# Where the sums of seven pairs stand: at step 2.65 of the next pair or directly ahead of its first values' group

## The chip, the cores and the metric

The kernel runs on one core of a Trainium2 chip. The metric is the device time of one execution in microseconds (us). The engines are named as in the profile: PE multiplies matrices (TensorE), PEld is its weight load, DVE is VectorE, ACT is ScalarE, POOL is GpSimd, and SP is the queue from which almost all transfers are issued. The chip's working memory (SBUF) and the accumulators (PSUM) have 128 partitions.

## The reference

The program is an attention with a bucket mask, followed by a feed-forward network with a rational function in place of the usual activation. Queries, keys and values have shape 4 x 8 x 768 x 64. Each query and each key gets a six-bit bucket, the signs of its product with `proj`; a query attends only to keys of its own bucket.

```python
mask = q_bucket[:, :, :, None] == k_bucket[:, :, None, :]
scores = np.where(mask, scale * np.matmul(q, k.transpose(0, 1, 3, 2)), -1e9)
attn = np.exp(scores - np.max(scores, axis=-1, keepdims=True))
attn = attn / (np.sum(attn, axis=-1, keepdims=True) + 1e-09)
x = np.matmul(attn, v)            # then 3072 tokens of 512 values
h = x @ w_in                      # 512 -> 2048
P = a[0] + a[1]*h + a[2]*h*h + a[3]*h*h*h
Q = 1.0 + np.abs(b[0])*np.abs(h) + np.abs(b[1])*h*h
out = (P / (Q + 1e-6)) @ w_out    # 2048 -> 512
```

## The kernel before

**Tiling.** The 32 heads (4 batches of 8) are worked on as 16 pairs; a pair's two heads share the 128 partitions, 64 each. A pair has 12 steps. Step s makes the scores of 128 keys against one half (384) of the queries, for both heads: half = s // 6, key tile = s % 6. Operands are kept as a rounded high part and a low part. Tile names of the profile: `pss` is scores, `psm` row maxima, `psb` bucket bits, `pst` a transpose of the maxima, `psv` values, `psu` sums, `psh` and `pso` the two products of the feed-forward part.

**One step.** `scores` issues, for each head, two matmuls into one of the three PSUM buffers of tag "s" in pool `ps_b`; ACT then writes exp(scores / 8) to one of seven tiles `E`. POOL adds the exps of three key tiles into a partial sum `acc`, so that a pair has four of these (two halves, `PARTS` = 2 each). `maxstep` belongs to the pair after the next: two matmuls into one of two buffers of `ps_a`, and a maximum by DVE. These maxima become the shift that is subtracted inside the scores.

**Values.** After six steps, `values` issues 24 matmuls for the six exps, 64 columns wide, the two heads side by side in the array. `values_out` copies one column (`col`) and moves the half's result, `xo`, out of PSUM on ACT; `values_store` writes it to memory.

**Sums.** `sums` multiplies the four partial sums by a matrix of ones: 8 products, 16 matmuls in the profile, each 32 columns wide and four of them beside each other in the array. They go to a buffer of tag "s"; ACT copies it to `sr`, and `sums_store` writes that to memory. Every fourth pair `recips` reads the sums of a batch back and makes reciprocals.

**Order.** Every operation of every engine is pinned to program order (`Ordered`). The order is made by a plan: `at(p, s, f, ...)` files a call under the key 12 p + s, where s may be a fraction and may run past 12 into the next pair; all calls are then made in order of their keys. `MID` holds the keys of the middle pairs, `FIRST` and `LAST` those of the first and the last. So sums at 14.65 of pair p are issued at step 2.65 of pair p + 1. In `MID`, per pair: values' groups at 5.66 and 11.05, values_out at 8.5 and 14.5 (step 2.5 of the next pair), the stores of xo at 9 and 15, bits at 2.81 in even pairs, the cast of the k of the pair after next at 1.19, a weight cast at 14.29 (step 2.29 of the next pair).

**Feed-forward part.** It begins in pair 15 and runs 6 blocks of 512 tokens by 16 slices of `w_in`'s columns. `gemm` makes `psh`, ACT, DVE and POOL make the rational function, and `gemm2`, four steps later, adds to `pso`. After a block, `store` writes four tiles of output rows, `o`. Up to then a block's next tokens are loaded, with products `y` in the buffers `lo0` and `lo1` of pool `raw`, which in the attention part hold the low parts of q and k.

Of the kernel before, what the change touches and what calls it, by code (L numbers as in the profile page):

```python
# [7 lines left out]
F32 = mybir.dt.float32  # L8
# [10 lines left out]
P = 128  # L19
S = 768  # L20
HQ = 384
# [4 lines left out]
NPAIR = B * NHP  # L26
NB = 6
TOK = B * S
DM = 512
# [6 lines left out]
CLAMP = 2.0 ** 40  # L36
PINNED = ("tensor", "vector", "scalar", "gpsimd", "sync")
PARTS = 2
ACCS = 5

MID = dict(
    group=6, values=[0.66, 0.05], values_out=3.5, maxima=7.17,
    maxima_steps=[0, 1.15, 1.73, 2.64, 3.32, 5.08, 5.86, 6.98, 8.0, 8.84, 10.26, 11.37], sums=14.65, sums_store=17.37,
    high=[-0.41, 1.19], low=[1.06, 3.35], bits=2.81, penalties=4.05, high_move=1.9, maskrows=5.61, second_low=-2.2,
    second_high=2.69, load_v=10.99, shift_turn=8.61, shift_rows=8.82, load=9.0, recips=[20.0, 22.0, 23.0],
    weights=[[1.44, 4.0, 4.1, 5.09, 5.49, 7.11, 9.5, 9.75, 17.5], [8.05, 10, 10.65, 11.5, 12.38, 14.29, 16.34, 19.32, 21.22]],
# [18 lines left out]
    sums=16.96, wide=8, share=11, third=0, sums14=14.69, weights14=1.44, sumst14=22.46,  # L65
# [8 lines left out]
class Ordered:  # L74


    def __init__(self, tc, engines=PINNED):
        self.tc, self.pinned = tc, engines
# [24 lines left out]
@with_exitstack  # L103
def bucket_attention_then_rational_ffn(ctx, tc, qT, kT, v, proj, w_in, w_out, coef, consts, out):
    nc = Ordered(tc)
    nc.scalar.preload_act_table_set("natural_log_exp_and_others")

    cpool = ctx.enter_context(tc.tile_pool(name="cpool", bufs=1))
    dpool = ctx.enter_context(tc.tile_pool(name="dpool", bufs=1, space=DRAM))
    wpool = ctx.enter_context(tc.tile_pool(name="wpool", bufs=1))  # L110


    raw = ctx.enter_context(tc.tile_pool(name="raw", bufs=2))
    ps_b = ctx.enter_context(tc.tile_pool(name="ps_b", bufs=1, space=PSUM))
    QF, KF = {}, {}

    def load(p, queue=nc.sync):
        both = raw.tile([P, 2, S], F32, tag="raw", name=f"qkf{p}")
        for t, (F, src) in enumerate(((QF, qT), (KF, kT))):
            F[p] = both[:, t, :]  # L120
            queue.dma_start(F[p], src[p])

    load(0)
    prj = cpool.tile([P, 2, 32], F32, name="prj")
    nc.scalar.dma_start(prj, proj)
    cst = cpool.tile([P, 2 + P], F32, name="cst")
    nc.scalar.dma_start(cst, consts)
    ident = cst[:, 2 : 2 + P]
    load(1)
    ones = cpool.tile([P, 32], F32, name="ones")  # L130
    nc.vector.memset(ones, 1.0)
    ab = cpool.tile([P, 6], F32, name="ab")
    a0, a1, a2, a3, b0, b1 = (ab[:, i : i + 1] for i in range(6))
    absb1 = cpool.tile([P, 1], F32, name="absb1")
    qbias = cpool.tile([P, 1], F32, name="qbias")
    nc.vector.memset(qbias, 1.0 + 1e-6)

    x_d = [dpool.tile([P, S], F32, name=f"x_d{i}") for i in range(NPAIR)]
    s_d = [dpool.tile([2 * NHP, S], F32, name=f"s_d{i}") for i in range(B)]
    r_d = [dpool.tile([2 * NHP, S], F32, name=f"r_d{i}") for i in range(B)]  # L140

    wo_d = [dpool.tile([P, 2, DM], F32R, name=f"wo_d{i}") for i in range(NFC)]

    wi_hi = wpool.tile([P, NCC, DFF], F32R, name="wi_hi")
    wi_lo = wpool.tile([P, NCC, DFF], F32R, name="wi_lo")

    tokens = Tokens(tc, nc, raw, x_d, r_d)
    gemm = Gemm1(nc, ps_b, tokens, wi_hi, wi_lo)
    tail = ctx.enter_context(tc.tile_pool(name="tail", bufs=1))

    def coefficients():
        nc.sync.dma_start(ab, coef)
        yield
        nc.scalar.activation(absb1, b1, AF.Abs)
        yield

    early = ExitStack()
    right = ctx.enter_context(ExitStack())
    ffn = Ffn(tc, nc, tokens, gemm, wo_d, (a0, a1, a2, a3, b0, absb1, qbias), tail, out)

    def operands_to_terms():
        early.close()
        ffn.terms_pool(right)
        tokens.last_rows = ffn.tp

    tail.tile([P, 32], F32, tag="below", name="below")
    last = attention(tc, nc, raw, ps_b, tail, tokens, early, operands_to_terms, ffn, load, QF, KF, v, w_in, w_out, wo_d, ident, cst,
                     ones, prj, wi_hi, wi_lo, x_d, s_d, r_d, coefficients)
    ffn.rest(ctx, last)
# [3 lines left out]
def attention(ctx, tc, nc, raw, ps_b, tail, tokens, early, operands_to_terms, ffn, load, QF, KF, v, w_in, w_out, wo_d, ident, cst, ones, prj,  # L173
# [215 lines left out]
    def values_out(p, hf):  # L389
        ps = AV.pop((p, hf))  # L390
        col = sm.tile([P, 1], F32, tag="col", name=f"col{p}_{hf}")
        xo = AV[p, hf] = tail.tile([P, DM], F32, tag="xo", name=f"xo{p}_{hf}", bufs=2)[:, 0:HQ]
        nc.scalar.copy(col, ps[:, HQ : HQ + 1])
        nc.scalar.activation(xo, ps[:, 0:HQ], AF.Identity, bias=col)

# [3 lines left out]
    def sums(p):  # L399
        ps = ps_b.tile([P, 512], F32, tag="s", bufs=3, name=f"psu{p}")  # L400
        for k in range(PARTS):
            for hf in range(2):
                acc = ACC.pop((p, hf, k))
                for h in range(2):
                    o = 64 * h + 32 * hf
                    nc.tensor.matmul(ps[o : o + 32, 0:HQ], ones, acc[:, h, :], start=(k == 0), stop=(k == PARTS - 1))
        ACC[p] = tail.tile([P, DM], F32, tag="sr", name=f"sr{p}")[:, 0:HQ]
        nc.scalar.copy(ACC[p], ps[:, 0:HQ])

    def sums_store(p):  # L410
# [65 lines left out]
    def at(p, s, f, *args):  # L476
        plan.setdefault(12 * p + s, []).append((f, args))
# [5 lines left out]
    for p in range(NPAIR):  # L483
        mid = 0 < p < NPAIR - 1
        n = MID["group"] if mid else (FIRST if p == 0 else LAST)["group"]
        for s in range(12):
            if p > 0 or s >= FIRST["ahead"]:
                at(p, s, scores, p, s)

            if p > 1:  # L490
                at(p - 2, MID["maxima"] + MID["maxima_steps"][s] if p > 2 else FIRST["maxima2"] + FIRST["rate2"] * s, maxstep, p, s)
            if s % n == n - 1:
                for i in range(s - n + 1, s + 1):
                    at(p, s + (MID["values"][s // n] if mid else (FIRST if p == 0 else LAST)["values"][s // n]), values, p, i)
            if s % NT == NT - 1:
                at(p, s + (LAST["vout14"] if (p, s) == (NPAIR - 2, 11) else MID["values_out"] if mid else (FIRST if p == 0 else LAST)["values_out"]), values_out, p, s // NT)
        for hf in range(2):
            at(p, 6 * hf + 9, values_store, p, hf)
        if p < NPAIR - 1:
            at(p, MID["sums"] if p < NPAIR - 2 else LAST["sums14"], sums, p)  # L500
            at(p, MID["sums_store"] if p < NPAIR - 2 else LAST["sumst14"], sums_store, p)
        if p > 1:
            for t in range(2):
                at(p - 2, (MID if p > 2 else FIRST)["high"][t], high, p, t)
                at(p - 2, (MID if p > 2 else FIRST)["low"][t], low, p, t, nc.vector if p > 2 else nc.gpsimd)
            if p % 2 == 0:
                at(p - 2, (MID if p > 2 else FIRST)["bits"], bits, p)
                at(p - 2, (MID if p > 2 else FIRST)["penalties"], penalties, p)
            at(p - 2, (MID if p > 2 else FIRST)["high_move"], high_move, p)
            at(p - 2, (MID if p > 2 else FIRST)["maskrows"], maskrows, p)  # L510
        if p > 0:
            at(p - 1, (MID if p > 1 else FIRST)["second_low"], second_low, p)
            at(p - 1, (MID if p > 1 else FIRST)["second_high"], second_high, p)
            at(p - 1, (MID if p > 1 else FIRST)["load_v"], load_v, p)
        if p > 1:
            at(p - 1, MID["shift_turn"], shift_turn, p)
            at(p - 1, MID["shift_rows"], shift_rows, p)
        if p > 3:
            at(p - 4, MID["load"], load, p)
        if p % NHP == NHP - 1 and p + 1 < NPAIR:  # L520
            spread(p, MID["recips"], recips(p // NHP))
# [12 lines left out]
    for f, x in enumerate(LAST["ffn"]):  # L534
        at(NPAIR - 1, x, ffn.step, f)
    at(NPAIR - 1, LAST["sums"], sums, NPAIR - 1)

    warm(12)
    K1[0] = operand("k1", 0, [P, 2, S], F32R, 3)
# [124 lines left out]
class Ffn:  # L664
# [1 line left out]

    LAG = 4

    def __init__(self, tc, nc, tokens, gemm, wo_d, coef, rows, out):
        self.tc, self.nc, self.tokens, self.gemm, self.wo_d, self.coef, self.out = tc, nc, tokens, gemm, wo_d, coef, out  # L670
        self.rows = rows
        self.state, self.sums = {}, {}
        self.done = 0

# [57 lines left out]
    def store(self, t, i, end, last):  # L732
        nc = self.nc
        if end and last:
            o = self.tp.tile([P, DM], F32, tag="h2", name=f"o{t}_{i}", bufs=2)
        else:
            tag, bufs = ("sr", 1) if i % 3 == 2 else ("xo", 2)
            o = self.rows.tile([P, DM], F32, tag=tag, name=f"o{t}_{i}", bufs=bufs)
        if end and i == 1:
            nc.vector.tensor_scalar(out=o, in0=self.sums[t, i], scalar1=-1.0, scalar2=None, op0=ALU.mult)  # L740
        else:
# [88 lines left out]
```

## Time and profile before

| | us |
|---|---|
| median of 3 runs (929.65 to 930.06) | 929.81 |
| the profiled execution, own time | 929.79 |
| its span in the profile | 928.0 |
| PE busy | 920.8 (99%) |
| DVE busy | 842.0 (91%) |
| ACT busy | 647.6 (70%) |
| POOL busy | 435.8 (47%) |

The attention part takes some 400 us, the feed-forward part the rest. A PE that is busy 99% does not work at its peak: matmuls are pipelined, a row's duration is longer than the distance to the next start, and starts tell more than durations. The granted clock is full in all forty slices. In rows of a timeline the first number is the start in us from the span's start and the second the time to the end of the last of the merged instructions; brackets hold idle time before it and what ended that.

### The profile page before, as it was taken

The page shows a single profiled execution, that of the slowest core. Times are in us where ns is not written, and L with a number is a line of the kernel's source. Part 1 is how long each engine was busy: PE and PEld are TensorE (multiplying, and loading weights), DVE is VectorE, ACT ScalarE, POOL GpSimd, SP SyncE. Part 2 cuts the span into 40 slices and gives each one's busy share as a digit, 9 for nine tenths or more (in the row PEclk, how much of TensorE's full clock was granted, in tenths as well). Part 3 has the DMA queues.
Part 4 walks back from the last instruction along what each step waited for, and adds up shares of the span by engine and source line. Part 5 has one row for each costly group of instructions (what it writes and reads, how often), then busy time and mean ns, then how long its engine had stood idle before and what let it go on. Part 6 is the DMA issues. An engine that isn't in the chain of part 4 may idle for free.

```text
span 928.0 us, 13694 instructions
## 1 busy us (share of the span) xinstructions
PE 920.8 (99%) x4678; PEld 699.9 (75%) x4678; DVE 842.0 (91%) x1029; ACT 647.6 (70%) x1229; POOL 435.8 (47%) x361
## 2 busy tenths in 40 slices
PE   8999999999999999999999999999999999999998
PEld 4666766666767676668888888888888888888886
DVE  6799889888988898888998999899999999998996
ACT  6567767676767766887767766776676677667664
POOL 5587878787788877622222232223222322232221
PEclk9999999999999999999999999999999999999999
DMA  6767878878877777545402100400040003001001
GB/s 197 214 181 219 229 230 230 223 214 212 242 212 225 229 195 233 163 155 197 163 1 81 56 1 1 136 2 0 1 137 1 1 34 102 1 1 46 1 1 46
DMA packets 51098, 111.57 MB, mean 120 GB/s; under 512 B 9330, under 2 KB 19942, under 8 KB 51028
## 3 DMA queue, kind: packets, MB, share of 16 engines
q1 hardware_dynamic: 50596, 110.34, 40.5%
q8 instruction: 37, 0.61, 0.3%
q10 hardware_dynamic: 432, 0.36, 0.1%
q14 instruction: 33, 0.27, 0.1%
HBM read 56.82 MB, written 21.17 MB: 84 GB/s over the span
## 4 chain that ended last, share of the span: by engine, by line
PE 93%; DVE 4%; DMA 1%; SPq 0%; ACT 0%; issue 0%; DVEq 0%; ACTq 0%
PE psh L93 28%; PE pso L93 28%; PE pss L93 14%; PE psv L93 12%; PE psm L93 7%; PE psu L93 2%; DVE m L93 2%; DMA wr<-w_in 1%; PE psb L93 1%; DVE ws L93 1%; DVE wr L93 0%; SPq L93 0%; PE psw L93 0%; PE pst L93 0%; ACT E L93 0%
## 5 line engine op out<-in xcount | busy, mean ns | idle before, releaser
L93 POOL TENSOR_TENSOR gl<-c,gh 128x512 fp32r<-128x512 f32 x95 | 133.2, 1402 | 387.0 <-ACT gh L93 371.0
L93 ACT ACTIVATE E<-pss 128x384 f32<-128x384 f32 x384 | 167.5, 493 | 105.8 <-PE pss L93 91.9
L93 PE MATMUL pso<-wo,gh 128*128 128x512 f32 x768 | 236.2, 390 | 0.0
L93 DVE TENSOR_REDUCE m<-psm 128x1 f32<-128x768 f32 x192 | 179.5, 948 | 31.4 <-PE psm L93 28.2
L93 POOL TENSOR_TENSOR acc<-E,E 128x384 f32<-128x384 f32 x124 | 155.6, 1273 | 85.9 <-ACT E L93 85.7
L93 PE MATMUL pss<-q,k 128*128 128x384 f32 (+2 forms) x768 | 171.3, 347 | 0.3 <-ACT E L93 0.3
L93 PEld LDWEIGHTS pso<-wo,gh 128*128 128x128 f32 x768 | 144.3, 188 | 29.9
L93 PEld LDWEIGHTS pss<-q,k 128*128 128x128 f32 (+2 forms) x768 | 134.6, 190 | 29.1 <-issue 17.0
L93 PE MATMUL psh<-xh,wi_hi 128*128 128x512 f32 x384 | 149.8, 390 | 0.0
L93 PE MATMUL psh<-xl,wi_hi 128*128 128x512 f32 x384 | 149.7, 390 | 0.0
L93 PE MATMUL psh<-xh,wi_lo 128*128 128x512 f32 x384 | 149.6, 390 | 0.0
L93 PE MATMUL pso<-wo,gl 128*128 128x512 f32 x384 | 149.1, 390 | 0.0
L93 ACT ACTIVATE h<-psh 128x512 f32<-128x512 f32 x96 | 57.4, 598 | 130.5 <-PE psh L93 130.3
L93 POOL TENSOR_TENSOR acc<-acc,E 128x384 f32<-128x384 f32 x123 | 136.6, 1129 | 5.9 <-ACT E L93 5.7
L93 DVE SCALAR_TENSOR_TENSOR c<-c,ab,r 128x512 f32<-128x512 f32 x96 | 135.6, 1413 | 0.0
L93 PE MATMUL psv<-E,v 128*64 128x385 f32 x768 | 131.9, 492 | 0.0
L93 PE MATMUL psm<-k,q 76*128 76x384 f32 (+1 forms) x384 | 102.4, 349 | 1.6 <-DVE m L93 1.0
L93 PEld LDWEIGHTS psv<-E,v 128*64 128x64 f32 x768 | 52.2, 137 | 65.3 <-issue 63.7
L93 DVE SCALAR_TENSOR_TENSOR w<-h,absb,w 128x512 f32<-128x512 f32 x96 | 74.0, 771 | 16.2 <-ACT w L93 15.9
L93 PEld LDWEIGHTS psh<-xh,wi_hi 128*128 128x128 f32 x384 | 72.1, 188 | 16.1 <-issue 1.2
L93 PEld LDWEIGHTS psh<-xh,wi_lo 128*128 128x128 f32 x384 | 72.2, 188 | 14.9
L93 PEld LDWEIGHTS psh<-xl,wi_hi 128*128 128x128 f32 x384 | 72.1, 188 | 14.9
(78 smaller groups left out, 1221.3 us busy)
## 6 DMA issues: line engine op xcount, KB each, us to landing
q<-q SPq DMA_DIRECT2D x45, 192.0 KB
k<-k SPq DMA_DIRECT2D x45, 192.0 KB
wr<-w_in SPq DMA_DIRECT2D x16, 512.0 KB
wr<-w_out SPq DMA_DIRECT2D x16, 512.0 KB
wo_d<-wr SPq DMA_DIRECT2D x16, 512.0 KB
wo<-wo_d SPq DMA_DIRECT2D x16, 512.0 KB
qkf<-qT SPq DMA_DIRECT2D x16, 384.0 KB
qkf<-kT SPq DMA_DIRECT2D x16, 384.0 KB
```

The lines of the kernel that those rows point to most:

```text
L93: return self.tc.keep_in_program_order(issue(*args, **kwargs))
```

## The change

In pairs 0, 2, ... 12 the sums move from key 14.65 to 17.65, that is from step 2.65 of the next pair to 5.65, where the first values' group follows at 5.66. The copy of the sums becomes a function of its own, filed at 17.67 for these pairs, and their store moves from 17.37 to 20.37. In the odd pairs all keys stay. For this a sixth buffer of partial sums is needed, since two of the next pair's are in use by step 5. Room is made: `xo` has one buffer of 384 columns for two of 512, `sr` 384 for 512, and the feed-forward part's output rows go to `lo0`, `lo1` and a new tile `row` instead.

```diff
-ACCS = 5
+ACCS = 6
...
-    ... sums=14.65, sums_store=17.37,
+    ... sums=[17.65, 14.65], sums_copy=[17.67, 14.65], sums_store=[20.37, 17.37],
...
-    ffn = Ffn(tc, nc, tokens, gemm, wo_d, (a0, a1, a2, a3, b0, absb1, qbias), tail, out)
+    ffn = Ffn(tc, nc, tokens, gemm, wo_d, (a0, a1, a2, a3, b0, absb1, qbias), raw, out)
...
-        xo = AV[p, hf] = tail.tile([P, DM], F32, tag="xo", name=f"xo{p}_{hf}", bufs=2)[:, 0:HQ]
+        xo = AV[p, hf] = tail.tile([P, HQ], F32, tag="xo", name=f"xo{p}_{hf}")
...
-        ACC[p] = tail.tile([P, DM], F32, tag="sr", name=f"sr{p}")[:, 0:HQ]
+        ACC[p] = ps
+
+    def sums_copy(p):
+        ps, ACC[p] = ACC[p], tail.tile([P, HQ], F32, tag="sr", name=f"sr{p}")
         nc.scalar.copy(ACC[p], ps[:, 0:HQ])
...
-            at(p, MID["sums"] if p < NPAIR - 2 else LAST["sums14"], sums, p)
-            at(p, MID["sums_store"] if p < NPAIR - 2 else LAST["sumst14"], sums_store, p)
+            early = p < NPAIR - 2
+            at(p, MID["sums"][p % 2] if early else LAST["sums14"], sums, p)
+            at(p, MID["sums_copy"][p % 2] if early else LAST["sums14"], sums_copy, p)
+            at(p, MID["sums_store"][p % 2] if early else LAST["sumst14"], sums_store, p)
...
+    at(NPAIR - 1, LAST["sums"], sums_copy, NPAIR - 1)
...
-            tag, bufs = ("sr", 1) if i % 3 == 2 else ("xo", 2)
-            o = self.rows.tile([P, DM], F32, tag=tag, name=f"o{t}_{i}", bufs=bufs)
+            pool, tag = (self.tp, "row") if i % 3 == 2 else (self.raw, f"lo{i % 3}")
+            o = pool.tile([P, DM], F32, tag=tag, name=f"o{t}_{i}", bufs=1)
```

More of the change, by code (lines that the diff above doesn't have):

```diff
@@ L38 @@
 PARTS = 2
-ACCS = 5
+ACCS = 6
 MID = dict(
     group=6, values=[0.66, 0.05], values_out=3.5, maxima=7.17,
-    maxima_steps=[0, 1.15, 1.73, 2.64, 3.32, 5.08, 5.86, 6.98, 8.0, 8.84, 10.26, 11.37], sums=14.65, sums_store=17.37,
+    maxima_steps=[0, 1.15, 1.73, 2.64, 3.32, 5.08, 5.86, 6.98, 8.0, 8.84, 10.26, 11.37], sums=[17.65, 14.65], sums_copy=[17.67, 14.65], sums_store=[20.37, 17.37],
     high=[-0.41, 1.19], low=[1.06, 3.35], bits=2.81, penalties=4.05, high_move=1.9, maskrows=5.61, second_low=-2.2,
@@ L667, with __init__ @@
     LAG = 4
-    def __init__(self, tc, nc, tokens, gemm, wo_d, coef, rows, out):
+    def __init__(self, tc, nc, tokens, gemm, wo_d, coef, raw, out):
         self.tc, self.nc, self.tokens, self.gemm, self.wo_d, self.coef, self.out = tc, nc, tokens, gemm, wo_d, coef, out
-        self.rows = rows
+        self.raw = raw
         self.state, self.sums = {}, {}
```

## The prediction

> **What bounds the kernel now.** I read the page first: the span, the chain that ended last by engine, and the costliest groups of ACT and DVE in the attention part.
>
> ```profile
> span 928.0 us, 13694 instructions
> PE 93%; DVE 4%; DMA 1%; SPq 0%; ACT 0%; issue 0%; DVEq 0%; ACTq 0%
> L93 ACT ACTIVATE E<-pss 128x384 f32<-128x384 f32 x384 | 167.5, 493 | 105.8 <-PE pss L93 91.9
> L93 DVE TENSOR_REDUCE m<-psm 128x1 f32<-128x768 f32 x192 | 179.5, 948 | 31.4 <-PE psm L93 28.2
> ```
>
> PE is the chain. So every microsecond taken from PE's stream is won, and every microsecond in which PE must wait is lost: nothing behind it has room to give it back. The two groups matter for their means: one exp takes 0.49 us of ACT, one row maximum 0.95 us of DVE.
>
> Then I went to the place of the change: PE's timeline in pair 3, where the sums of pair 2 stand today (the columns are start, duration, group).
>
> ```profile
> 100.62 0.52 PE L93 MATMUL psm<-k,q 76*128 76x384 f32 x2
> 101.07 1.50 PE L93 MATMUL psu<-acc,ones 128*32 128x384 f32 x16
> 102.50 0.98 PE L93 MATMUL pss<-q,k 77*128 77x384 f32 x4
> 103.32 0.52 PE L93 MATMUL psm<-k,q 76*128 76x384 f32 x2
> 103.67 0.87 PE L93 MATMUL pss<-q,k 77*128 77x384 f32 x4
> ...
> 105.89 4.10 PE L93 MATMUL psv<-E,v 128*64 128x385 f32 x24
> ```
>
> Read the starts, not the durations. Two maxima matmuls take 0.35 us (103.32 to 103.67), but 0.45 us when the narrow sums follow (100.62 to 101.07): entering a narrow shape costs 0.10. The four score matmuls behind the sums take 0.82 (102.50 to 103.32), where four take 0.71 elsewhere (364.63 to 365.34, in the rows on a stall below): leaving costs 0.11 there. The sums hold PE 1.43 (101.07 to 102.50).
>
> **What the change removes from PE.** In seven pairs (0, 2, ... 12) the sums leave step 2.65 of the next pair and stand at 5.65, right ahead of the 24 values matmuls at 5.66. One entry and one exit between a wide and a narrow shape go. What a change from 32 to 64 columns costs is shown once, where the bits of pair 1 (32 columns) are followed by values (64); beside it two groups of 32 columns in a row.
>
> ```profile
> 33.91 1.50 PE L93 MATMUL psb<-qkf,prj 128*32 128x384 f32 x16
> 35.33 1.51 PE L93 MATMUL psv<-E,v 128*64 128x385 f32 x8
> ...
> 124.13 1.50 PE L93 MATMUL psu<-acc,ones 128*32 128x384 f32 x16
> 125.44 1.47 PE L93 MATMUL psb<-qkf,prj 128*32 128x384 f32 x16
> ```
>
> Sixteen 32-column matmuls take 1.42 before a 64-column group, 1.31 before one of their own shape, 1.43 before a wide one. So the sums will hold PE 1.42 ahead of the values, and a move saves 0.10 (entry) + 0.11 (exit) + 0.01 = 0.22; if the change of shape were free, 0.33. Times seven: 1.5 us, at most 2.3.
>
> [...]
>
> **What the move takes away from ACT.** Step 2.65 is not an empty place. Here is ACT in the same stretch.
>
> ```profile
> 99.47 0.87 ACT L93 ACTIVATE E<-pss 128x384 f32<-128x384 f32 x2 [0.20 <-PE pss L93]
> 100.22 0.83 ACT L93 CAST k<-qkf 128x768 fp32r<-128x768 f32 x1
> 100.95 0.88 ACT L93 ACTIVATE E<-pss 128x384 f32<-128x384 f32 x2
> 101.70 0.64 ACT L93 CAST wr<-ws 128x512 fp32r<-128x512 f32 x1
> ...
> 102.43 0.58 ACT L93 ACTIVATE xo<-psv,col 128x384 f32<-128x384 f32 x1
> 102.91 0.47 ACT L93 COPY sr<-psu 128x384 f32<-128x384 f32 x1
> ```
>
> From 99.47 to 102.91 ACT never waits: two exps, the cast of k, two exps, a weight cast, the column copy and the move of xo. Today PE spends 1.43 us of this in the sums and so does not ask for the next exps. With the sums gone it does, and scores have three PSUM buffers, two tiles a step: a step's second tile needs the buffer of the previous step's first tile, so that tile's exp must be done about one step (1.06 us of PE) after it was made. The trace has a case where it is not, in pair 14.
>
> ```profile
> 364.63 0.88 PE L93 MATMUL pss<-q,k 77*128 77x384 f32 x4
> 365.34 0.51 PE L93 MATMUL psm<-k,q 76*128 76x384 f32 x2
> 365.70 1.14 PE L93 MATMUL pss<-q,k 77*128 77x384 f32 x4
> 366.67 0.34 PE L93 MATMUL psm<-k,q 76*128 76x384 f32 x1
> 365.66 0.88 ACT L93 ACTIVATE E<-pss 128x384 f32<-128x384 f32 x2
> ```
>
> The exp of the first tile of 364.63 runs 365.66 to 366.15; the four score matmuls from 365.70 then take 0.97 instead of 0.71. Of the 0.26, about 0.16 is the wait of the second tile (due 0.35 after 365.70, released about 0.05 after the exp's end) and 0.10 the weight load that a held matmul no longer hides, as at a change of shape.
>
> Now pair 3 without the sums at 2.65. Score step 3 starts at 100.97 (100.62 + 0.35). Its exps stand behind xo in ACT's order, so the first cannot start before 102.91 (the slot that the copy sr had) and ends at 103.40. The second tile of step 4 would be due at 100.97 + 1.06 + 0.35 = 102.38; it starts at 103.45. From there to the values: the rest of that tile with its exposed weight load 0.46, maxima 0.35, scores of step 5 0.71, maxima and entry 0.45, sums 1.42 = 3.39. Values at 106.84 instead of 105.89: **+0.95**. Values start 4.41 after xo's start (0.48 + 0.49 + 0.05 + 3.39), whatever PE did earlier. Pairs 7, 9, 11 have the same ACT rows; the last of them, and the rows that decide the other three:
>
> ```profile
> 292.77 0.58 ACT L93 ACTIVATE xo<-psv,col 128x384 f32<-128x384 f32 x1
> 296.22 0.55 PE L93 MATMUL psv<-E,v 128*64 128x385 f32 x2
> 150.62 1.81 DVE L93 TENSOR_REDUCE m<-psm 128x1 f32<-128x768 f32 x2
> 153.41 0.55 PE L93 MATMUL psv<-E,v 128*64 128x385 f32 x2
> 341.09 1.81 DVE L93 TENSOR_REDUCE m<-psm 128x1 f32<-128x768 f32 x2
> 343.74 0.54 PE L93 MATMUL psv<-E,v 128*64 128x385 f32 x2
> 55.41 0.96 DVE L93 TENSOR_REDUCE m<-psm 128x1 f32<-128x768 f32 x1
> 56.88 0.88 PE L93 MATMUL pss<-q,k 77*128 77x384 f32 x4
> 57.69 0.55 PE L93 MATMUL psv<-E,v 128*64 128x385 f32 x2
> ```
>
> Pair 11: 292.77 + 4.41 = 297.18 against 296.22, +0.96; so the four pairs 3, 7, 9, 11 give 3.8. In pairs 5 and 13 DVE decides. The maximum of step 2 is the first of the pair at 150.62 and ends at 151.57; step 4's maxima matmuls need its buffer (two buffers), start at 151.62, and from there stand 0.46 + 0.71 + 0.45 + 1.42 = 3.04 to the values: 154.66 against 153.41, +1.25. Likewise 341.09 + 0.95 + 0.05 + 3.04 = 345.13 against 343.74, +1.39. In pair 1 DVE already paces PE: the reduction of 55.41 ends at 56.37 with or without the sums, and holds the last maxima matmuls, so the scores start at 56.88 as now, the sums at 57.69, the values 1.42 later: +1.42, the sums having cost nothing where they stood.
>
> **The rest.** The sums' new place makes the stretch without maxima 1.4 us longer; DVE and ACT, both behind by then, catch up, and stalls in the half behind it may go. How much, no row tells. I take 0.8 back, a tenth of what the weight loads of maxima wait for DVE today (first row below); the bounds are 0 and 1.5.
>
> ```profile
> PEld psm L93 <- DVE m L93: 8.8, 28, 0.6
> 104.42 0.94 SPq L93 DMA_DIRECT2D x_d<-xo  x1
> 113.94 0.58 ACT L93 ACTIVATE xo<-psv,col 128x384 f32<-128x384 f32 x1
> 503.68 0.60 ACT L93 ACTIVATE o<-pso 128x512 f32<-128x512 f32 x1 [1.20 <-DMA out<-o]
> ```
>
> The copy sr itself (0.47) moves into the values block, where ACT waits for scores. Its two DMAs move in SP's queue from behind x_d to behind the w_out load, past the four mask-row moves; nobody needs them before the reciprocals in the next pair. The sixth partial sum adds no instruction. One xo buffer for two: ACT's next xo comes 8.58 us after the previous store's issue ended (104.42 + 0.94 to 113.94), so it costs nothing unless a store takes that long. Output rows: the row that waits today for the first row's store (503.68) waits the same, since lo0 returns at the fourth row as xo did; the other users of these buffers, the products y of the next tokens, are made two FFN steps later. It is the same wait on the same store, so FFN is put at zero.
>
> **Sum.** 3.8 + 1.25 + 1.39 + 1.42 = 7.9, less 0.8, gives +7.1 on the profiled execution's 929.79 (span 928.0): **936.9 us**, slower by 0.8%. The median, 929.81, is the same to 0.02. The 1.5 us of saved shape changes is inside these numbers, since they go from start to start.
>
> **Rivals.** (1) *Only the shape changes count.* ACT's and DVE's lateness is taken up elsewhere and PE keeps its pitch: 929.8 - 1.5 = 928.3. For it: PE shows almost no idle time today. Against: the wait of pair 14. Decides if the exps of step 3 start by 101.85 or so; ACT's row says 102.91. (2) *The same, and 32 to 64 columns is free behind sums*: 929.8 - 2.3 = 927.5. Against it the 1.42. (3) *The single xo buffer holds ACT.* From a landing over 8.6 us; each half microsecond beyond, in the 15 halves of pairs like this one and with about 0.25 us of slack, adds some 4 us: 941. Against: with quiet queues the store awaited at 503.68 landed in some 2 us.
>
> **Chances.** Forecast 0.80, rival 1 0.07, rival 2 0.07, rival 3 0.06. A measurement of this kernel tells about 0.2% (1.9 us) from no change. Faster 0.07 (rival 2), the same 0.07 (rival 1), slower 0.86. The range of the forecast: ACT's terms alone without DVE's give 7 x 0.9 less 1.5, +4.8; everything without relief +7.9; with some 1.2 either way for what the trace does not show, 933.4 to 939.0, and rivals 1 to 3 stay outside.
>
> **What would show it.** Right: in pairs 3 to 13 (odd) the sums directly ahead of values, 1.42 before them; values 4.4 us behind xo's start; PE's weight loads of pss waiting for exps over 4 us more in total; step 3's exps starting behind xo; FFN's length unchanged. Wrong: no gap inside the scores of step 4, values 0.2 us earlier than now, or exps of step 3 ahead of xo.

## The result and the profile after

The changed kernel takes 940.93 us (median of 5 runs, 938.03 to 941.70) against 930.06 us for the kernel before beside it: a ratio of 1.011, 95% interval 1.0093 to 1.0126. It is slower, as forecast, but by 10.9 us instead of 7.1, and outside the range. The profiled execution took 941.49 us, with a span of 939.6.

These are the lines of the page after that answer to those shown of before, with the groups of the scores' and the maxima's matmuls beside them (busy, mean ns | idle before them and what ended most of it):

```profile
span 939.6 us, 13715 instructions
...
PE 92%; DVE 3%; DMA 2%; ACT 1%; issue 1%; SPq 0%; POOL 0%; DVEq 0%; ACTq 0%; POOLq 0%
...
L93 ACT ACTIVATE E<-pss 128x384 f32<-128x384 f32 x384 | 167.5, 493 | 109.6 <-PE pss L93 106.9
...
L93 DVE TENSOR_REDUCE m<-psm 128x1 f32<-128x768 f32 x192 | 179.5, 949 | 41.6 <-PE psm L93 38.2
...
L93 PE MATMUL pss<-q,k 128*128 128x384 f32 (+2 forms) x768 | 174.8, 349 | 2.9 <-ACT E L93 2.7
...
L93 PE MATMUL psm<-k,q 76*128 76x384 f32 (+1 forms) x384 | 103.0, 351 | 4.7 <-DVE m L93 4.0
```

The same two groups of PE in the page before:

```profile
L93 PE MATMUL pss<-q,k 128*128 128x384 f32 (+2 forms) x768 | 171.3, 347 | 0.3 <-ACT E L93 0.3
...
L93 PE MATMUL psm<-k,q 76*128 76x384 f32 (+1 forms) x384 | 102.4, 349 | 1.6 <-DVE m L93 1.0
```

One exp and one maximum cost what they did (493 and 949 ns). What is new is that PE waits for them: 2.7 us for exps instead of 0.3, 4.0 for maxima instead of 1.0. The sign that the forecast named, PE's weight loads of `pss` waiting over 4 us more for exps, is there too: 8.0 us in all instead of 1.2. But it is not enough: PE's own new waits are 5.4 us, against 11.6 us of span.

Where the time went is read from the starts of the values' groups, each against its start before. A shift that grows between two starts was added there; between the places listed it drifts by 0.06 at most. Shifts are taken from unrounded starts.

| values' group of | start before | start after | shift | added here | predicted |
|---|---|---|---|---|---|
| pair 0, second half | 46.92 | 45.95 | -0.97 | -0.97 | 0 |
| pair 1 | 57.69 | 59.61 | +1.93 | +2.90 | +1.42 |
| pair 3 | 105.89 | 108.75 | +2.86 | +0.95 | +0.95 |
| pair 5 | 153.41 | 157.54 | +4.13 | +1.24 | +1.25 |
| pair 7 | 200.94 | 205.97 | +5.03 | +0.95 | +0.95 |
| pair 7, second half | 212.29 | 216.96 | +4.68 | -0.35 | part of -0.8 |
| pair 9 | 248.87 | 254.49 | +5.63 | +0.95 | +0.95 |
| pair 11 | 296.22 | 302.82 | +6.60 | +0.97 | +0.96 |
| pair 13 | 343.74 | 353.30 | +9.56 | +2.94 | +1.39 |
| pair 13, second half | 354.61 | 364.35 | +9.74 | +0.18 | part of -0.8 |
| pair 14 | 367.11 | 377.54 | +10.42 | +0.69 | 0 |
| pair 14, second half | 376.73 | 388.20 | +11.47 | +1.04 | 0 |
| end of the last matmul | | | +11.49 | +0.02 | 0 |

Five of the seven moves cost what the working said, to 0.02 us. Two cost twice as much, and pair 14, which the change doesn't touch, loses 1.7. The lead of 0.97 in pair 0 isn't the change's either. At the start of an execution PE's first matmuls (`psw`, whose results are not used) stand 0.32 us apart, and 0.16 us once the full clock begins; that is at 4.51 us here and at 7.15 in the execution before, which the forty slices of either page don't show. Two other traces fit: counted back from their half-clock windows at 202.11 (ACT cleared) and 251.66 (kept busy) in steps of 3.4133 us (below), the full clock began at 4.14 and 5.90 by estimate, and pair 0's first values' group starts at 40.0 and 40.6 there, at 39.9 here and at 40.9 before.

Pair 3 is the model of the five. PE's timeline after, from the scores of step 4 on (the same columns as in the prediction), and below it ACT's:

```profile
104.24 0.52 PE L93 MATMUL pss<-q,k 77*128 77x384 f32 x2
105.36 0.62 PE L93 MATMUL pss<-q,k 77*128 77x384 f32 x2 [0.60 <-ACT E L93]
105.81 0.52 PE L93 MATMUL psm<-k,q 76*128 76x384 f32 x2
106.17 0.87 PE L93 MATMUL pss<-q,k 77*128 77x384 f32 x4
106.88 0.52 PE L93 MATMUL psm<-k,q 76*128 76x384 f32 x2
107.33 1.50 PE L93 MATMUL psu<-acc,ones 128*32 128x384 f32 x16
108.75 4.10 PE L93 MATMUL psv<-E,v 128*64 128x385 f32 x24
```

```profile
103.61 0.64 ACT L93 CAST wr<-ws 128x512 fp32r<-128x512 f32 x1
104.12 0.19 ACT L93 COPY col<-psv 128x1 f32<-128x1 f32 x1
104.34 0.58 ACT L93 ACTIVATE xo<-psv,col 128x384 f32<-128x384 f32 x1
104.82 1.74 ACT L93 ACTIVATE E<-pss 128x384 f32<-128x384 f32 x4
```

The four exps stand right behind xo; the first ends at about 105.31, and at 105.36 the second score tile of step 4 begins, after 0.60 us in which PE had nothing. Values start 108.75 - 104.34 = 4.41 us after xo, as worked out; the sums stand 1.42 ahead of them.

Pair 1 is different. PE's timeline after:

```profile
53.04 0.62 PE L93 MATMUL psm<-k,q 76*128 76x384 f32 x2 [0.48 <-DVE m L93]
...
55.37 0.73 PE L93 MATMUL psm<-k,q 76*128 76x384 f32 x2 [0.65 <-DVE m L93]
55.90 1.48 PE L93 MATMUL pss<-q,k 77*128 77x384 f32 x4
57.31 2.37 PE L93 MATMUL psu<-acc,ones 128*32 128x384 f32 x16
59.61 2.81 PE L93 MATMUL psv<-E,v 128*64 128x385 f32 x16
```

The scores start at 55.90, which is the forecast's 56.88 less the 0.97 by which this execution is ahead. But they take 1.41 to the sums instead of 0.81, and the sums 2.30 to the values instead of 1.42. No wait is noted there. The reason is in the view by stretches, cut at the places where the granted clock changes (columns: stretch, length, then busy time and count of PE, PEld, DVE, ACT and POOL, the granted clock, DMA share, GB/s):

```profile
52.30:55.71 3.41, 2.28 (x12) 1.70 (x11) 3.41 (x5) 2.34 (x6) 3.02 (x4) 1.00 0.92 231
55.71:59.13 3.42, 3.42 (x18) 1.75 (x20) 3.42 (x6) 2.17 (x5) 3.42 (x3) 0.50 1.01 223
...
345.85:349.26 3.41, 2.81 (x12) 1.80 (x12) 3.41 (x5) 3.37 (x10) 3.41 (x3) 1.00 0.99 278
349.26:352.67 3.41, 3.41 (x19) 2.04 (x21) 3.41 (x5) 1.84 (x4) 3.41 (x4) 0.50 0.89 210
...
103.50:106.91 3.41, 2.81 (x15) 2.48 (x16) 3.41 (x5) 3.37 (x9) 3.41 (x3) 1.00 1.04 285
```

For 3.41 us in pair 1 and again in pair 13 PE ran at half its clock; everywhere else between the start and the end it had the full one. The page's forty slices don't show it: a slice is 23.5 us long, and 3.4 of them at half speed leave the mean above nine tenths.

### The profile page after: what moved, and what is told of

The parts are those of the page before. It is cut to its first block, busy times and chain, and to the rows that moved or that the text cites. A ratio compares the mean times of both kernels' runs of the same rounds, so it can differ in the third digit from the quotient of the medians.

```text
span 939.6 us, 13715 instructions
## 1 busy us (share of the span) xinstructions
PE 926.3 (99%) x4678; PEld 699.7 (74%) x4678; DVE 842.5 (90%) x1029; ACT 648.7 (69%) x1229; POOL 438.6 (47%) x361
## 4 chain that ended last, share of the span: by engine, by line
PE 92%; DVE 3%; DMA 2%; ACT 1%; issue 1%; SPq 0%; POOL 0%; DVEq 0%; ACTq 0%; POOLq 0%
PE psh L93 28%; PE pso L93 28%; PE pss L93 13%; PE psv L93 13%; PE psm L93 7%; PE psu L93 2%; DVE m L93 2%; PE psb L93 1%; DMA k<-k 1%; ACT E L93 1%; SPq L93 0%; DVE ws L93 0%; DMA qkf<-qT 0%; DMA xh<-r_d 0%; PE pst L93 0%
## 5 line engine op out<-in xcount | busy, mean ns | idle before, releaser
L93 POOL TENSOR_TENSOR acc<-E,E 128x384 f32<-128x384 f32 x124 | 151.3, 1239 | 94.6 <-ACT E L93 94.4
L93 PE MATMUL pss<-q,k 128*128 128x384 f32 (+2 forms) x768 | 174.8, 349 | 2.9 <-ACT E L93 2.7
L93 POOL TENSOR_TENSOR acc<-acc,E 128x384 f32<-128x384 f32 x123 | 143.2, 1183 | 6.4 <-ACT E L93 6.2
```

The costliest lines, as they stand in the source:

```text
L93: return self.tc.keep_in_program_order(issue(*args, **kwargs))
```

## The experiments

**The changed kernel again.** Nothing is edited; the question is whether the half clock belongs to the kernel or to one execution.

> The changed kernel once more, for a second trace. Theory (the half clock is a second price of the new waits): the granted clock again falls to one half for whole windows of some 3.4 us, in pairs 1 and 13 where PE waits longest, and a run's time goes with the number of these windows: none about 938, each one up to 1.7 us more. Rival (the half-clock windows of the first trace were a disturbance): clock 1.0 throughout, about 938. In both, values start 0.95 later, pair against pair, in pairs 3, 7, 9, 11. Open: whether pair 14's 1.7 us, a wait for the tokens' transfer, comes again.

Measured: 941.80 us (938.82 to 944.47, 6 runs), ratio 1.0114, interval 1.0091 to 1.0138. The profiled run again has the half clock twice, in pair 1 from 56.22 and in pair 13 from 349.77, 3.413 us each, and the additions +2.91 and +2.92 there. The mean clock of the runs tells the rest, since two such windows lower it by 2 x 3.413 x 0.5 / 939 = 0.0036. Over both calls the kernel ran eleven times: the three runs with a mean clock of 0.999 took 938.03, 938.82 and 939.34 us, one with 0.998 took 940.59, and the seven with 0.994 to 0.996 took 940.93 to 944.47. Without the half clock the kernel takes some 938.7 us. One cost of this trace is new: pair 9 adds 1.43 instead of 0.95, where DVE's custom operation on the weights took 1.27 us instead of 0.68.

**Buffers only.** The sums go back to their old place; the six partial sums, the single xo and the output rows in `lo0`, `lo1` and `row` stay.

```diff
-    ... sums=[17.65, 14.65], sums_copy=[17.67, 14.65], sums_store=[20.37, 17.37],
+    ... sums=[14.65, 14.65], sums_copy=[14.65, 14.65], sums_store=[17.37, 17.37],
```

> The change with the sums left where they were (keys 14.65 and 17.37 in all pairs): six partial sums, one xo buffer, output rows in the low parts' buffers. Theory (all of the loss comes from the sums' new place): 929.8 to 930.3, the same as before, no xo that waits for a store, feed-forward part of the same length. Rival (the single xo buffer or the new buffers of output rows cost something): some 932 to 934, with ACT waiting for a store of xo or PE for pair 14's tokens.

Measured: 931.44 us, ratio 1.0008, interval 0.9999 to 1.0017: the same. No ACT instruction waits for a store of xo, so the rival of the single xo buffer falls, and the feed-forward part keeps its length. The interval leaves room for 1.6 us more at most. Its trace is 0.54 late in pair 1, 0.87 in pair 7 and 0.75 in pair 14, and nowhere else. In pairs 1 and 7 it is transfers that are waited for, in pair 14 a slice of w_in (below); that the new buffers delay them is not shown. DVE's timeline in pair 7:

```profile
197.31 1.58 DVE L93 TENSOR_TENSOR lo<-qkf,q 128x768 fp32r<-128x768 f32 x1 [1.17 <-DMA q<-lo]
```

**Five pairs.** Only the sums of pairs 2 to 10 move, so pairs 1 and 13 are as before.

```diff
+            k = p % 2 if 0 < p < 12 else 1
-            at(p, MID["sums"][p % 2] if early else LAST["sums14"], sums, p)
+            at(p, MID["sums"][k] if early else LAST["sums14"], sums, p)
```

(The copy and the store follow the same k, here and in the experiments below.)

> The change without its first and last pair: only the sums of pairs 2, 4, 6, 8, 10 move. Theory: pairs 3, 7, 9, 11 pay 0.95 each, pair 5 pays 1.25, pair 7's second half gives 0.35 back: 929.9 + 4.7 = 934.6, clock 1.0, because a stretch with waits like theirs keeps PE busy enough. Rival (the clock falls as soon as PE waits at all): half-clock windows here too, 936 to 938. If pair 14's late tokens come from pair 12's sums and their store in SP's queue, pair 14 is as before here; if from all that came earlier, or by chance, 935 to 936.

Measured: 935.62 us, ratio 1.0056, interval 1.0036 to 1.0077. Full clock throughout in the profiled run. Pairs 3, 5, 7 and 11 add 0.94, 1.26, 0.94 and 0.95, pair 7's second half gives back 0.35; pair 9 adds 1.40, where DVE's custom operation on the weights took 1.25 us instead of 0.68, pair 13's second half 0.57 and pair 14's 0.28. Pair 1 adds nothing, pair 13's first half neither. The parts of ACT and DVE are thus a matter of the move alone, pair by pair. But one of the six runs took 940.79 us at a mean clock of 0.996, so the clock fell in that run too, though no trace shows where: the full clock that was expected with waits like these did not hold in every run.

**The two ends only.** The other side of it: only the sums of pairs 0 and 12 move.

```diff
+            k = 0 if p in (0, 12) else 1
```

> The complement of five_pairs: only the sums of pairs 0 and 12 move, those of 2 to 10 stay. Theory: pair 1 pays 1.4 and pair 13 pays 1.4, each 1.5 more in an execution where a half-clock window falls on it; pairs 3 to 11 as before; behind pair 13's values the 0.2 and in pair 14 the 0.7 appear, as in every trace so far with pair 12's sums moved and in none without. 929.9 + 2.8 + 0.9 = 933.6, up to 936.7 with two windows. Rival for pair 14 (its late tokens come from all the lateness before): pair 14 as before, 932.7 to 935.8.

Measured: 934.80 us, ratio 1.0042, interval 1.0029 to 1.0055. The profiled run has no half clock, and here pair 1 adds 1.34 and pair 13 1.41: the predicted 1.42 and 1.39. Pair 7's second half adds 0.33, pair 13's 0.19 and pair 14's 1.14; the 0.7 expected of pair 14's first half did not come. The other four runs have a mean clock of 0.998, what one half-clock window leaves, and took 934.36 to 935.01 us, no longer than the profiled one (934.50). No trace shows where their windows fell, so a window's price elsewhere stays open. PE of the profiled run in pair 1:

```profile
54.02 0.62 PE L93 MATMUL psm<-k,q 76*128 76x384 f32 x2 [0.48 <-DVE m L93]
...
56.35 0.62 PE L93 MATMUL psm<-k,q 76*128 76x384 f32 x2 [0.64 <-DVE m L93]
56.81 0.87 PE L93 MATMUL pss<-q,k 77*128 77x384 f32 x4
57.62 1.50 PE L93 MATMUL psu<-acc,ones 128*32 128x384 f32 x16
59.04 3.13 PE L93 MATMUL psv<-E,v 128*64 128x385 f32 x18
```

The waits are the same as in the changed kernel, 0.48 and 0.64 us, in the same places; only the clock differs. Term by term the half clock cost (55.90 - 55.37) - (56.81 - 56.35) = 0.07 at the maxima, 1.41 - 0.81 = 0.60 at the scores and 2.30 - 1.42 = 0.88 at the sums, together 1.55.

Why here and not there? In the changed kernel's trace the changes of the clock lie on a raster: those at 55.71, 59.13, 349.26 and 352.67 stand 15, 16, 101 and 102 steps of 3.4133 us behind 4.51, where the full clock began. In the two ends' kernel it began at 6.79 and kept to the end; if the same steps are counted from there, they cut pair 1 elsewhere. Its stretches between raster points, and those of the kernel of the next experiment:

```profile
51.17:54.58 3.41, 2.93 (x14) 1.93 (x14) 3.41 (x5) 3.18 (x9) 3.41 (x3) 1.00 0.61 159
54.58:57.99 3.41, 2.77 (x21) 2.00 (x23) 3.41 (x6) 1.58 (x4) 3.02 (x3) 1.00 1.00 229
...
341.30:344.71 3.41, 2.80 (x13) 1.91 (x12) 3.41 (x5) 3.37 (x10) 3.41 (x4) 1.00 0.99 220
```

```profile
51.93:55.34 3.41, 2.34 (x12) 1.67 (x10) 3.41 (x7) 2.30 (x7) 3.26 (x3) 1.00 0.84 227
...
198.70:202.11 3.41, 1.37 (x7) 0.86 (x6) 2.21 (x3) 1.96 (x5) 3.41 (x4) 1.00 1.05 270
202.11:205.52 3.41, 3.35 (x12) 2.62 (x16) 3.41 (x4) 0.00 (x0) 1.78 (x2) 0.50 1.00 227
```

With the raster of the changed kernel both waits of pair 1 fall into one window, whose rows fill 2.28 of 3.41 us; in the two ends' kernel they are parted over two, 2.93 and 2.77. But that is no rule: 2.81 was followed by the half clock in pair 13 and not in pair 3 of the same execution, 2.80 was not in pair 13 of the two ends' kernel, and 2.34 was not in the kernel below, though its window holds the first wait of pair 1 and 0.60 us of the second. Pair 9 of the five pairs' kernel has two waits, of 0.40 and 0.19 us, in one window, as pair 13 of the changed kernel has, and keeps the full clock behind it:

```profile
246.51:249.92 3.41, 2.82 (x13) 1.94 (x12) 3.41 (x5) 3.37 (x9) 3.41 (x4) 1.00 1.05 265
```

What decides between them stays open.

**ACT cleared.** The sums of all seven pairs are moved, and in the first steps of the odd pairs ACT gets room: the cast of k goes to the end of the pair before, a weight cast with its low part behind step 5.

```diff
-                at(p - 2, (MID if p > 2 else FIRST)["high"][t], high, p, t)
+                at(p - 2, -0.40 if t and p % 2 and p > 4 else (MID if p > 2 else FIRST)["high"][t], high, p, t)
...
+        if i % 4 == 1 and 1 < i < 26:
+            w[5:7] = [17.68, 17.69]
```

> The change, and in odd pairs two ACT casts taken out of the steps that the sums left: the cast of k goes from step 1.19 to ahead of the pair's first step, the weight cast from 2.29 to 5.68, behind the values (pairs 3 to 13). Theory (ACT's queue is what holds PE in pairs 3, 7, 9, 11): the exps of step 3 start 0.9 earlier, values there start within 0.1 of where they did before the change instead of 0.95 later; pairs 1, 5 and 13 keep their loss, which is DVE's. Total 3.7 us below the changed kernel's 940.9, that is 937, and 934 if no half-clock window falls. Rival (PE is held by something else there, by DVE's maxima or by the transfers): pairs 3, 7, 9, 11 stay at 0.95 and the time at 941.

Measured: 938.39 us, ratio 1.0083, interval 1.0066 to 1.01. In pairs 3, 9 and 11 the addition falls from 0.95 to 0.40, 0.40 and 0.44: ACT's share is shown (one DVE operation, the weights' low part, moved with the casts), and a second limit stands 0.5 us behind it, so the expected 0.1 was missed. So was the 934 without half clock: the run with a mean clock of 1.000 took 937.41. Pairs 1 and 13 add 1.35 and 1.41, with the full clock. Pair 7 adds 4.83. PE's rows of pairs 3 and 7:

```profile
103.62 0.62 PE L93 MATMUL psm<-k,q 76*128 76x384 f32 x2 [0.19 <-DVE m L93]
...
202.17 1.01 PE L93 MATMUL psm<-k,q 76*128 76x384 f32 x2 [2.10 <-DVE m L93]
```

In pair 3 it is now DVE that PE waits for. In pair 7 DVE's low part of q starts 1.41 us late (most likely for the moves of the previous `lo`, as in the trace of the buffers alone), the maxima behind it hold PE for 2.10, and two windows of half clock follow (202.11 to 208.94, in the stretches above). So here one late start cost its own time and that of two windows at half clock, most of pair 7's 4.83.

**Keep busy.** The changed kernel with extra matmuls of a constant ahead of the awaited maxima of pairs 1 and 13, whose result nobody reads. The question is whether the clock stays full where PE works instead of waiting.

```diff
+    def fill(n):
+        ps = ps_b.tile([P, 512], F32, tag="v", name=f"psf{len(WARM)}")
+        WARM.append(n)
+        for _ in range(n):
+            nc.tensor.matmul(ps[:, 0:P], ident, ident, start=True, stop=True)
+
+    for p, s, n in ((1, 3.235, 3), (1, 4.875, 3), (13, 3.165, 3), (13, 4.005, 1)):
+        at(p, s, fill, n)
```

> The changed kernel with a few extra matmuls of a constant, whose result nobody reads, ahead of the maxima that PE waits for in pairs 1 and 13 (three, three, three and one). They fill the wait, they do not shorten it. Theory (the clock falls to half because PE idles too much of a window there): no half-clock window, pairs 1 and 13 at +1.4 each instead of +2.9, 938 and less spread. Rival (the windows come from something else, or the fill delays PE more than it holds the clock): windows as before, 941 or more.

Measured: 938.82 us, ratio 1.0088, interval 1.0074 to 1.0101: 2 to 3 us below the changed kernel, whose interval overlaps a little. In the trace pair 1 adds 1.41 with the full clock. Pair 13 has the full clock too, but adds 2.15, because the extra matmuls waited for a PSUM buffer that xo had to free. A window of half clock shows up in pair 9 instead, where DVE's custom operation was long again (1.27 us), and makes it +2.94. PE's rows of pairs 13 and 9:

```profile
348.69 0.94 PE L93 MATMUL psf<-cst 128*128 128x128 f32 x6 [0.95 <-ACT xo L93]
...
249.36 0.62 PE L93 MATMUL psm<-k,q 76*128 76x384 f32 x2 [0.40 <-DVE m L93]
...
251.09 0.62 PE L93 MATMUL psm<-k,q 76*128 76x384 f32 x2 [0.19 <-DVE m L93]
...
253.50 2.25 PE L93 MATMUL psu<-acc,ones 128*32 128x384 f32 x16
```

Two waits of 0.40 and 0.19 us in one window: just what pair 13 has in the changed kernel, and also what pair 9 of the five pairs' kernel has, where the clock stayed full. Three of the four runs have a mean clock of 1.000, against 0.999 at most in the eleven of the changed kernel. That fits the theory, but one trace doesn't prove that the filling held the clock: pairs 1 and 13 kept it without any in the two ends' kernel and with ACT cleared.

**Cleared further, without and with the move.** Can the shape changes be cashed in if DVE has room as well? Beside what was cleared for ACT, the low part of q goes from 1.06 to 5.60 and the column copy a step ahead of xo. The first kernel moves no sums, the second those of pairs 2, 6, 8 and 10 (the last two lines below, against the first kernel).

```diff
+                odd = p % 2 and p > 4
+                at(p - 2, 5.60 if not t and odd else (MID if p > 2 else FIRST)["low"][t], low, p, t, nc.vector if p > 2 else nc.gpsimd)
...
-            k = 0 if p < 0 else 1
+            k = 0 if p in (2, 6, 8, 10) else 1
```

> No sums moved (keys 14.65 everywhere), the change's buffers, and in odd pairs 3 to 11 the first steps emptied: the cast of k goes from step 1.19 to ahead of the pair, the weight cast from 2.29 to 5.68, DVE's low part of q from 1.06 to 5.60, and the column copy goes one step ahead of xo. A base for the next kernel. All theories: about 930 to 931, as before; if DVE falls behind after the values group, up to 1 us more in each of these pairs.

> cleared_base with the sums of pairs 2, 6, 8, 10 moved to directly ahead of the first values' group. Theory (the move saves 0.2 us of shape changes, and only what ACT and DVE have to do in the emptied steps takes it away): pairs 3, 7, 9, 11 now start their values 0.2 earlier than in cleared_base, where the changed kernel started them 0.95 later; 0.8 us in all, under what a timing can tell, so the traces decide. Rival (PE's pitch suffers for another reason, as transfers or PSUM): these pairs still later than in cleared_base, by 0.3 to 0.9 each, 1 to 4 us in all.

Measured: 974.57 and 973.82 us, ratios 1.0475 (1.046 to 1.0489) and 1.0459 (1.0445 to 1.0474) to the kernel before. The first expectation failed by 44 us: the late low part of q delays the move of the mask rows behind it, and the maxima of the next but one pair wait for them, for example in pair 3's second half of the second kernel:

```profile
113.89 0.59 PE L93 MATMUL psm<-k,q 76*128 76x384 f32 x2 [2.31 <-DMA k<-mb]
```

Each such wait (six in either kernel, 17.0 and 15.3 us in all) is followed by two to four windows of half clock (mean clock 0.966 and 0.968); wait and windows cost 4.3 to 7.4 us a pair. The comparison that the two kernels were made for still stands, since these waits come later in the pair: the values of pairs 3, 7 and 11 start 0.18, 0.20 and 0.20 us earlier than where no sums are moved. The saving of shape changes is real: 0.2 us a move, as worked out (0.22). Pair 9 does not show it; it is 0.7 late there, where PE waits 0.67 us for DVE's maxima.

**Mended, without and with the move.** The low part of q back at its place, an operation of DVE on the weights moved behind step 5 instead.

```diff
-            w[5:7] = [17.68, 17.69]
+            w[4:7] = [17.665, 17.68, 17.69]
```

> No sums are moved. In the odd pairs 3 to 11 the first steps are emptied of ACT's cast of k and of the weight slice's casts on ACT and DVE, which go behind step 5, and the one-column copy is made a step ahead of xo; the low parts of q and k stay at their old keys, so the mask rows are as early as before. Theory (the 44 us of the earlier emptied kernel came from the late low part of q): values groups of pairs 3, 7, 9 and 11 begin within 0.1 us of their old distance to the start of the attention part, no half-clock window, no wait of row maxima for the mask rows; 930 to 932. Rival (a full ACT and DVE at step 5 holds PE there): the second halves of the odd pairs lose 0.5 us or more each, 933 or more.

> The same, and the sums of pairs 2, 6, 8 and 10 moved ahead of the values. Theory (a move gains the two changes of shape, 0.2 us, once ACT and DVE have room; it costs only where they have none): values groups of pairs 3, 7, 9 and 11 begin 0.2 us earlier than in the kernel without moved sums, 0.8 us in all, a ratio to it just under what can be told. Rival (the room made is not enough, as where only ACT was cleared): they begin 0.2 to 0.4 us later each, and the kernel is 1 to 2 us slower than the one without moved sums.

Measured: 937.55 and 936.52 us, ratios 1.0073 (1.0055 to 1.0092) and 1.0064 (1.0051 to 1.0077); neither beats the kernel before. The room was not free: without moved sums the second halves of the odd pairs 3 to 11 lose 0.7 to 1.1 us each. In pair 3 PE waits for an exp there, which stands behind the weight cast that was put off:

```profile
112.47 0.62 PE L93 MATMUL pss<-q,k 77*128 77x384 f32 x2 [0.77 <-ACT E L93]
```

With moved sums the first halves of pairs 3 and 11 gain nothing and lose nothing, those of pairs 7 and 9 lose 0.9, waiting 0.83 and 0.85 us for DVE's maxima behind a low part of q that starts 0.61 late for a transfer (pair 7) or takes 1.63 us instead of 0.95 (pair 9). PE of pair 3 with the move, and DVE:

```profile
101.73 0.89 PE L93 MATMUL pss<-q,k 77*128 77x384 f32 x4
102.55 0.62 PE L93 MATMUL psm<-k,q 76*128 76x384 f32 x2
103.00 0.87 PE L93 MATMUL pss<-q,k 77*128 77x384 f32 x4
```

```profile
101.54 1.82 DVE L93 TENSOR_REDUCE m<-psm 128x1 f32<-128x768 f32 x2
```

The scores of 101.73 take 0.82 and the maxima of 102.55 take 0.45, where 0.71 and 0.35 are free of waits: 0.21 us for two maxima and a low part in a row on DVE, as much as the shape changes gave. Of the first expectation the rival held (a full ACT and DVE behind step 5); of the second neither did: in pairs 3 and 11 gain and new wait cancel, pairs 7 and 9 lose more than the rival said, and yet the kernel with moved sums is not the slower one.

## Why the prediction was wrong in size

**Right: the direction and its mechanism.** The price of a move is the room that the old place gave to ACT and DVE, and it is lost where it was said. The terms of ACT (pairs 3, 7, 9, 11: 0.95, 0.95, 0.95, 0.97) and of DVE in pair 5 (1.24) came out to 0.02, and ACT's fell to 0.4 in pairs 3, 9 and 11 when ACT was cleared. Those of pairs 1 and 13 are 1.34 and 1.41 when the clock is full.

**Right: the shape changes.** Sums stand 1.42 us ahead of the values in pair 3 above and in pair 1 with the full clock (57.62 to 59.04), against 1.31 ahead of a group of their own 32 columns (124.13 to 125.44 before), so the change from 32 to 64 columns is not free here, and rival 2 falls. A move gains 0.2 where nothing else is in the way (0.18 to 0.20 in pairs 3, 7 and 11 of the cleared kernels). Rival 1 falls with the waits, 2.7 and 4.0 us, and rival 3 with the kernel with the buffers alone.

**Right: what was put at zero.** The buffers alone can't be told from the kernel before, no store holds xo, and the feed-forward part adds 0.02.

**Wrong: the terms for pairs 1 and 13**, 1.42 and 1.39. This is the step that failed: DVE's wait was right, but the matmuls behind it were priced at the full clock, and the range's 1.2 "for what the trace does not show" had no case for anything else. Measured 2.90 and 2.94: 3.0 us more than said, the half clock. What brings it in one execution and not in another stays open.

**Wrong in size: the relief of 0.8.** The trace gives back 0.35 in pair 7 and takes 0.18 in pair 13: 0.17 in all instead of 0.8. The quantity that I took a tenth of, the waits of the maxima's weight loads for DVE, grew instead of shrinking:

```profile
PEld psm L93 <- DVE m L93: 12.6, 32, 1.1
```

**Not in the sum: pair 14**, +1.7 us after, 1.2 in the second trace of the same kernel and 0 to 1.1 in the others (leaving aside the two cleared kernels, where half-clock windows reach up to it). Its second half can be followed: ACT waits for a slice of w_in, and what is lost is that wait less some 1.5 us. ACT's rows of the kernel before, the changed kernel, the two ends', the five pairs' and the one kept busy, in this order:

```profile
367.77 0.70 ACT L93 ACTIVATE ws<-wr 128x512 f32<-128x512 f32 x1 [1.24 <-DMA wr<-w_in]
```

```profile
379.49 0.69 ACT L93 ACTIVATE ws<-wr 128x512 f32<-128x512 f32 x1 [2.67 <-DMA wr<-w_in]
```

```profile
372.40 0.68 ACT L93 ACTIVATE ws<-wr 128x512 f32<-128x512 f32 x1 [2.64 <-DMA wr<-w_in]
```

```profile
372.90 0.69 ACT L93 ACTIVATE ws<-wr 128x512 f32<-128x512 f32 x1 [1.76 <-DMA wr<-w_in]
```

```profile
377.69 0.68 ACT L93 ACTIVATE ws<-wr 128x512 f32<-128x512 f32 x1 [1.05 <-DMA wr<-w_in]
```

Waits of 2.67, 2.64 and 1.76 go with losses of 1.04, 1.14 and 0.28; 1.24 and 1.05 with none. What makes the slice land later stays open: the kernel kept busy has the whole change and the shortest wait, the kernel with the buffers alone has 2.20, and there is one trace of the kernel before. On this evidence it can't be called a cost of the moved sums. The first half's 0.69 is a wait of 0.73 us for a maximum that stands behind DVE's first product y of the feed-forward tokens, which starts 0.89 us after the operation before it. The second trace and the kernel with ACT cleared have the same; the one kept busy has no such pause and loses nothing. What holds y stays open.

**The account.** 7.1 predicted, + 3.0 for the half clock, + 0.6 for the relief (0.8 less 0.35 and 0.18 lost), + 1.7 in pair 14, - 1.0 by which this execution's full clock began earlier, is 11.4; the end stands at +11.49. Without the half clock this sum would be 8.4, 1.3 more than the forecast; that it isn't 2.3 more is the early clock of this execution, and so luck.

## What to carry to other kernels

A short group of matmuls that looks misplaced may be the time in which the other engines catch up: before it is moved, add up their work from the last free moment to the next operand that PE asks for, and price the move by that. Where PE is paced by another engine already, look at the granted clock too: here windows of 3.41 us at half clock followed waits of 0.48 and 0.65 us in pair 1, and of 0.41 and 0.19 in pair 13, and cost some 1.5 us each. Look for them in stretches as short as these windows, since slices of 23.5 us hid them. And room made by putting work off had to be paid here where the work then stood, with 0.77 us for an exp behind a weight cast and 2.31 for mask rows: what waits behind it, transfers first, comes into the sum.

## What the hardware showed unasked

In the changed kernel's trace the granted clock fell to 0.50 for two windows of 3.413 us, with PE's rows filling two thirds to four fifths of the window before (2.28 and 2.81 of 3.41), and this cost about 1.5 us in the two places where the same pair can be compared with and without it: 1.55 in pair 1, 2.94 - 1.41 = 1.53 in pair 13, a little less than half a window. It differs from one execution of the same kernel to the next (mean clock 0.994 to 0.999). That the raster decides, by gathering two waits in one window or parting them, fits pair 1 in the two kernels compared, but pair 1 with ACT cleared and pair 9 of the five pairs' kernel speak against it. The time covered by rows does not tell the two cases apart: the window filled to 1.37 was followed by two at half clock, but of those at 2.3 to 2.8 some were and others were not. What decides stays open.
